# The last unit's softmax sums in four column tiles, with reciprocals spread by transfers

## The chip, the cores and the metric

The kernel runs on one core of one Trainium2 chip. Time is device time in microseconds (us) of one launch; a kernel's time is the median of its runs. Besides, one execution was recorded by the hardware profiler; its rows give start and length of every instruction. The engines are named as the profile names them: PE is TensorE (PEld its weight loads), ACT is ScalarE, DVE is VectorE, POOL is GpSimd, SP is the sequencer that issues most DMAs.

## The reference

Attention with normalised q and k, and behind it a two-layer network with a leaky ReLU. 8 batches, 12 heads, 448 rows, 64 columns; the network takes 3584 tokens of width 768 to 2048 and back.

```python
def _attn_ref(q, k, v, g_q, g_k):
    def rmsnorm(x, g):
        rms = np.sqrt(np.mean(x * x, axis=-1, keepdims=True) + 1e-06)
        return x / rms * g
    q_n, k_n = (rmsnorm(q, g_q), rmsnorm(k, g_k))
    scores = (1.0 / np.sqrt(q.shape[-1])) * np.matmul(q_n, k_n.transpose(0, 1, 3, 2))
    scores = scores - np.max(scores, axis=-1, keepdims=True)
    attn = np.exp(scores)
    attn = attn / (np.sum(attn, axis=-1, keepdims=True) + 1e-09)
    return np.matmul(attn, v)

def _moe_ref(x, w_in, w_out):
    h = x @ w_in
    g = np.maximum(0.01 * h, h)
    return g @ w_out
```

Inputs and outputs are float32; x is the attention's output with the heads of a token side by side.

## The kernel before

The attention is cut into 24 units, each one batch and four of its twelve heads: unit u is group u % 3 of batch u // 3. A unit's scores are computed transposed in seven steps of 64x64 tiles (`qk`, L195), and ScalarE turns each step into exponentials `et` in fp16 (`ex`, L214). Two results are then taken from `et`: the softmax sums and the products with v. Each unit writes its third of `xts[b]`, the network's input x for its batch.

There are two ways to the sums and reciprocals.

- The wide way (units 0 to 3 and the last one, 23): `zsum_slot` (L265) multiplies `et` by ones in 64x64 tiles, 28 matmuls of 448 columns, so that the sums come out already repeated over the 64 rows of each head; `zinv` (L326, L327) takes logarithm and exponential with a minus sign on 128x896; `xmul` (L349) multiplies by the products straight out of PSUM on VectorE, in two halves.
- The narrow way (units 4 to 22): `zcol` (L283) takes 28 matmuls of 224 columns in four column tiles of 32, so that each sum stands in 16 rows only; `zcol_ln` (L300) and `zcol_inv` (L305) work on 128x224; four DMAs on SP (L310) then repeat the reciprocals `zs` over the rows of `rz`; `pv_out` (L295) copies the products from PSUM to `x32`, and `xmul_pool` (L320) multiplies `x32` by `rz` on GpSimd (`xmul_sb` is the same multiply on VectorE).

The network's work stands in `queue`, a list of items (a closure and a cost each). Between the attention's steps `fill` runs items by cost. Each batch adds its items with `push`. After the last unit all that is left is run in order. An item may leave VectorE or ScalarE work for afterwards with `later`; the next item begins with `flush`, which emits it, so such work stands on its engine behind the item's own matmuls.

Around the end the order on PE is this: the first four items i0 to i3 of `seven`, which computes two tiles of batch 6's output by seven products instead of eight (L444, eight matmuls each, most with an add or copy by VectorE or ScalarE behind them), the last unit's sums and products, items i4, i5, i6, and then batch 7 with `late1`, which does the like for the first layer (L564). Its items (n, s), six matmuls each, run in the order of `LATE_ALL`:

```python
    LATE_ALL = ((1, 0), (2, 0), (7, 0), (1, 1), (6, 0), (7, 1), (1, 2), (5, 0), (4, 0), (6, 1), (3, 0), (2, 1), (7, 2), (5, 1),
```

Item n = 1 reads x of the older units only, n = 2 and n = 3 read the last unit's x, n = 4 to 7 read the sums `xs[4]`, `xs[1]`, `xs[2]`, `xs[3]`. VectorE makes those in `x_sum` (L550): 3 and 1 first, then 2 and 4; 2 needs 1, and 4 needs 2. Behind the items VectorE and ScalarE add up the parts (L577, L612, L581) and apply the leaky ReLU (L574). Item (6, 0) accumulates into the PSUM bank of (1, 0), VectorE adds that bank to the one of (7, 0), and (5, 0) accumulates into the same bank again:

```python
            elif n == 6:
                mm(g[1, s], 6, s, xs[2], False)
                later(lambda: vadd(g[7, s][:, 0:S], g[1, s], tmp["v"][:, s % 2]))
            elif n == 5:
                mm(g[1, s], 5, s, xs[1], False)
```

PSUM has four banks for all this (`aux`, handed round in a list while `hold` is on) and two slots of two banks for scores, which `late1` takes over, one bank of each.

Of the kernel before, what the change touches and what calls it, by code (L numbers as in the profile page):

```python
# [18 lines left out]
def kernel(  # L19
# [13 lines left out]
    B, H, S, D = q.shape  # L33
# [4 lines left out]
    NU = B * NQ  # L38
# [18 lines left out]
    def aux(shape, dtype, name):  # L57
        if held:
            return held[0].pop(0)
        return psum.tile(shape, dtype, tag="aux", bufs=4, name=name)  # L60
# [6 lines left out]
    def drop(bank):  # L67
        if held:
            held[0].append(bank)
# [119 lines left out]
    def slot():  # L189
        return psum.tile([P, 2, 512], FP32, tag="sT", bufs=2, name="sT")  # L190
# [69 lines left out]
    def zsum(u, t0=0, t1=NS):  # L260
        s = st[u]
        for t in range(t0, t1):
            for r in range(2):
                for a in range(2):
                    nc.tensor.matmul(s["zt"][r][64 * a:64 * a + 64, 0:S], ones16[64 * r:64 * r + 64],  # L265
                                     s["et"][64 * r:64 * r + 64, t, a], start=(t == 0), stop=(t == NS - 1))

    def zsum_slot(u):
        s = st[u]
        s["zslot"] = slot()  # L270
        s["zt"] = [s["zslot"][:, r] for r in range(2)]
        zsum(u)
# [3 lines left out]
    def zcol(u):  # L276
        s = st[u]
        s["zc"] = aux([P, 512], FP32, "zc")
        for t in range(NS):
            for y in range(2):  # L280
                for a in range(2):
                    c = 32 * (2 * y + a)
                    nc.tensor.matmul(s["zc"][c:c + 32, 0:HS], onesr, s["et"][:, t, a, HS * y:HS * y + HS],  # L283
                                     start=(t == 0), stop=(t == NS - 1))

    def pv_slot(u):
        s = st[u]
        s["pslot"] = slot()
        s["pv"] = [s["pslot"][:, r] for r in range(2)]
        pv(u)  # L290

    def pv_out(u):
        s = st[u]
        s["x32"] = zpool.tile([P, 2, S], FP32, tag="x32", name="x32")
        nc.scalar.copy(s["x32"], s["pslot"][:, :, 0:S])  # L295

    def zcol_ln(u):
        s = st[u]
        s["zs"] = zpool.tile([P, HS], FP32, tag="zs", name="zs")
        nc.scalar.activation(s["zs"], s["zc"][:, 0:HS], AF.Ln)  # L300
        drop(s["zc"])

    def zcol_inv(u):
        s = st[u]
        nc.scalar.activation(s["zs"], s["zs"], AF.Exp, bias=0.0, scale=-1.0)  # L305
        s["rz"] = zpool.tile([P, 2, S], FP32, tag="rz", name="rz")
        for r in range(2):
            for y in range(2):
                src = s["zs"][64 * y + r:64 * y + 64:2, None, :]
                nc.sync.dma_start(s["rz"][:, r, HS * y:HS * y + HS], src.broadcast_to([32, 4, HS]))  # L310

    def xmul_sb(u):
        xmul_pool(u, nc.vector)

    def xmul_pool(u, eng=nc.gpsimd):
        s = st[u]
        b, g = divmod(u, NQ)
        if b not in xts:
            xts[b] = xpool.tile([P, NQ, 2, S], FP16, tag="xt", name="xt")
        eng.tensor_tensor(xts[b][:, g], s["x32"], s["rz"], op=ALU.mult)  # L320

    def zinv(u):
        s = st[u]
        s["rz"] = zpool.tile([P, 2, S], FP32, tag="rz", name="rz")
        if "zslot" in s:
            nc.scalar.activation(s["rz"], s["zslot"][:, :, 0:S], AF.Ln)  # L326
            nc.scalar.activation(s["rz"], s["rz"], AF.Exp, bias=0.0, scale=-1.0)  # L327
        else:
            for r in range(2):
                nc.scalar.activation(s["rz"][:, r], s["zt"][r][:, 0:S], AF.Ln)  # L330
                nc.scalar.activation(s["rz"][:, r], s["rz"][:, r], AF.Exp, bias=0.0, scale=-1.0)

    def pv(u, t0=0, t1=NS):
        s = st[u]
        if t0 == 0 and "pslot" not in s:
            s["pv"] = [aux([P, 512], FP32, "pv") for r in range(2)]
        for t in range(t0, t1):
            for r in range(2):
                for a in range(2):
                    nc.tensor.matmul(s["pv"][r][64 * a:64 * a + 64, 0:S], vts[u % NV][64 * r:64 * r + 64, a, t],  # L340
                                     s["et"][64 * r:64 * r + 64, t, a], start=(t == 0), stop=(t == NS - 1))

    def xmul(u):
        s = st[u]
        b, g = divmod(u, NQ)
        if b not in xts:
            xts[b] = xpool.tile([P, NQ, 2, S], FP16, tag="xt", name="xt")
        for r in range(2):
            nc.vector.tensor_tensor(xts[b][:, g, r], s["pv"][r][:, 0:S], s["rz"][:, r], op=ALU.mult)  # L349
            drop(s["pv"][r])  # L350
# [85 lines left out]
    def later(fn, *args):  # L436
        pend.append(lambda: fn(*args))
# [97 lines left out]
    def x_b(b, i, j):  # L535
        v_ = xts[b].rearrange("p g r (t x) -> p (g r) t x", t=NS)
        return v_[:, HK * i:HK * i + HK, :, 32 * j:32 * j + 32]

    def x_tiles():
        if not xs:  # L540
            two = [prep_p.tile([P, 2, HK, HX], FP16, tag="sq", bufs=3, name="xs") for i in range(2)]
            for n in range(1, 5):
                xs[n] = two[n // 3][:, (n - 1) % 2].rearrange("p k (t x) -> p k t x", t=NS)

    def x_sum(b, n):
        x_tiles()
        t = xs
        a, c = {1: (x_b(b, 0, 1), x_b(b, 0, 0)), 2: (x_b(b, 1, 1), t[1]),
                3: (x_b(b, 1, 1), x_b(b, 0, 1)), 4: (x_b(b, 1, 0), t[2])}[n]
        nc.vector.tensor_tensor(t[n], a, c, op=ALU.subtract)  # L550
# [87 lines left out]
    queue = []  # L638

    def also(fn, *more):  # L640
        def both():
            fn()
            for m in more:
                m()
        return both
# [56 lines left out]
    def fill(u, d, jobs):  # L702
        total = sum(c for c, _ in queue)
        left = WD[d] + 3.0
        uu, dd = u, d
        while True:
            dd += 1
            if dd == 4:
                uu, dd = uu + 1, 0
            if uu == NU or (fed(uu, dd) and (u > 3 or uu > 3)):  # L710
                break
            left += WD[dd]
        debt[0] += total * WD[d] / left
        while queue and debt[0] >= queue[0][0] * 0.5:
            c, fn = queue.pop(0)
            fn()
            debt[0] -= c
            if jobs:
                jobs.pop(0)()
        flush()  # L720
        for job in jobs:
            job()
# [21 lines left out]
    with tc.manual_schedule():  # L744
# [182 lines left out]
        for u in range(3, NU):  # L927
            for d in range(4):
# [75 lines left out]
                    for ti in range(2):  # L1004
                        job(prep_sq, u + 3, ALL, (ti,))
                fill(u, d, jobs)
        zsum_slot(NU - 1)
        pv(NU - 1)
        zinv(NU - 1)
        xmul(NU - 1)  # L1010
        for i, ns in enumerate(((3, 1), (2, 4))):
            c, fn = queue[i]
            queue[i] = (c, also(fn, *[lambda n=n: later(x_sum, B - 1, n) for n in ns]))
        push(B - 1)
        while queue:
            queue.pop(0)[1]()
# [29 lines left out]
```

## Time and profile before

| | us |
|---|---|
| median of 8 runs | 421.68 |
| lowest and highest run | 420.77, 422.46 |
| the profiled execution's own time | 421.3 |
| its span, first to last instruction | 419.5 |
| TensorE busy | 403.2 (96%) |
| ScalarE busy | 303.8 (72%) |
| VectorE busy | 270.2 (64%) |
| granted TensorE clock | 1.0 |

A row of a timeline gives the start from the span's beginning, the length, the engine, the line of the kernel, the operation, what it writes and reads, shapes, and how many instructions are merged in the row. Brackets give idle time of the engine just ahead and what ended it. Rows of TensorE overlap a little, since matmuls are pipelined; the distance from one row's start to the next is what a group costs. "SPq" rows are DMA issues: their length is the sequencer's time, and not the transfer's.

### The profile page before, as it was taken

What the parts mean: (1) busy time and instruction counts of PE and PEld (TensorE: products, weight loads), DVE (VectorE), ACT (ScalarE), POOL (GpSimd) and SP (SyncE); (2) the same over time, 40 slices, a digit from 0 to 9 for tenths busy, and PEclk for the clock granted to TensorE, in tenths of its full rate; (3) what the DMA queues carried; (4) which work ended last, traced back from release to release, by engine and by line L of the source; (5) the groups of instructions that cost most, each with busy time, mean ns of one, the idle gap of its engine ahead of it and who ended that gap; (6) DMA issues with size and microseconds to landing.
All of it is one profiled execution on the core that took longest, in us unless ns stands there. A gap on an engine that the chain in (4) does not pass through costs nothing.

```text
span 419.5 us, 9568 instructions
## 1 busy us (share of the span) xinstructions
PE 403.2 (96%) x3959; PEld 222.9 (53%) x3959; DVE 270.2 (64%) x440; ACT 303.8 (72%) x474; POOL 83.1 (20%) x75
## 2 busy tenths in 40 slices
PE   8787999999999999999999999999999999999995
PEld 7454444545445544555455544455445557558863
DVE  5888675887568837566448735467338787527762
ACT  5999877768887689767986779967986657653600
POOL 1968422200020112210121120120101101010000
PEclk9999999999999999999999999999999999999999
DMA  7999997889664795677664796578552460032023
GB/s 262 226 251 256 238 251 115 208 151 211 157 155 74 215 236 104 162 182 166 154 140 91 204 202 143 157 147 179 163 108 44 121 157 8 8 76 75 2 53 99
DMA packets 71951, 62.42 MB, mean 149 GB/s; under 512 B 36324, under 2 KB 67044, under 8 KB 71908
## 3 DMA queue, kind: packets, MB, share of 16 engines
q1 hardware_dynamic: 61312, 49.62, 46.2%
q0 software_dynamic: 10272, 11.80, 17.7%
q8 instruction: 31, 0.51, 0.5%
q10 hardware_dynamic: 324, 0.39, 0.3%
q14 instruction: 12, 0.10, 0.1%
HBM read 45.61 MB, written 11.01 MB: 135 GB/s over the span
## 4 chain that ended last, share of the span: by engine, by line
PE 83%; ACT 9%; DVE 6%; issue 1%; DVEq 0%; ACTq 0%
PE hps L362 27%; PE sT L195 8%; PE sT L340 6%; ACT et L214 6%; PE ma L444 5%; PE md L444 5%; PE mc L444 5%; PE bank L444 5%; PE bank L564 4%; PE op L403 3%; PE zc L283 3%; PE mb L444 3%; PE warm L742 2%; PE sT L444 2%; DVE n L167 1%
## 5 line engine op out<-in xcount | busy, mean ns | idle before, releaser
L214 ACT ACTIVATE et<-sT,eb 128x896 f16<-128x896 f32 x166 | 159.6, 1011 | 18.6 <-PE sT L195 16.8
L362 PE MATMUL hps<-xt,win 128*128 128x448 f16 x600 | 120.8, 353 | 0.2 <-DVE xt L349 0.2
L362 PEld LDWEIGHTS <-win 128*128 128x128 f16 x612 | 56.8, 98 | 58.2 <-issue 9.6
L320 POOL TENSOR_TENSOR xt<-x,rz 128x896 f16<-128x896 f32 x16 | 33.4, 2085 | 148.7 <-DMA rz<-zs 131.5
L167 DVE TENSOR_TENSOR n<-rq,rinv 128x896 f16<-128x896 f32 (+2 forms) x25 | 28.1, 1127 | 49.7 <-ACT rinv L161 47.0
L356 ACT ACTIVATE gt<-hps 128x448 f16<-128x448 f32 x100 | 54.1, 557 | 6.0 <-PE hps L362 5.4
L195 PE MATMUL sT<-qkT 64*64 64x448 f16 x664 | 52.4, 363 | 4.6 <-ACT et L214 3.6
L155 DVE TENSOR_REDUCE ssq<-sq 128x14 f32<-128x896 f32 (+2 forms) x49 | 50.4, 1058 | 1.1 <-ACT sq L144 1.1
L444 PEld LDWEIGHTS <-sa 128*128 128x128 f16 x352 | 32.8, 98 | 26.3 <-issue 6.1
L295 ACT COPY x<-sT 128x896 f32<-128x896 f32 x19 | 17.2, 906 | 36.4 <-DVE sT L245 36.4
L124 POOL DMA_DIRECT2D vt<-in_v_dram x24 | 18.2, 759 | 114.2 <-PE sT L340 106.7
L195 PEld LDWEIGHTS <-qkT 64*64 64x64 f16 x672 | 15.5, 104 | 37.8 <-issue 34.2
L444 PEld LDWEIGHTS <-gt 128*128 128x128 f16 x264 | 25.2, 98 | 18.8 <-issue 2.4
L340 PE MATMUL sT<-et,vt 64*64 64x448 f16 x532 | 28.5, 349 | 0.3
L403 PE MATMUL op<-wout,gt 128*128 128x384 f16 x160 | 28.4, 327 | 0.0
L340 PEld LDWEIGHTS <-vt 64*64 64x64 f16 x672 | 20.7, 107 | 11.3 <-issue 1.7
L232 DVE TENSOR_REDUCE sT<-sT 128x1 f32<-128x896 f32 x22 | 24.0, 1093 | 4.0 <-PE sT L195 4.0
L167 DVE TENSOR_TENSOR n<-rk,rinv 128x896 f16<-128x896 f32 (+2 forms) x26 | 26.1, 1011 | 0.0
L403 PEld LDWEIGHTS <-gt 128*128 128x128 f16 x192 | 17.6, 98 | 14.3 <-issue 3.0
L444 PE MATMUL ma<-wout,gt 128*128 128x384 f16 x128 | 23.5, 326 | 0.0
L425 DVE TENSOR_TENSOR sa<-gt 128x512 f16<-128x512 f16 (+1 forms) x15 | 8.2, 544 | 18.6 <-ACT gt L356 14.0
L144 ACT ACTIVATE sq<-rq 128x896 f32<-128x896 f32 (+2 forms) x18 | 16.3, 913 | 1.0 <-DMA rq<-in_q_dram 1.0
(135 smaller groups left out, 515.9 us busy)
## 6 DMA issues: line engine op xcount, KB each, us to landing
rq<-in_q_dram SPq DMA_DIRECT2D x24, 448.0 KB, 3.8
rk<-in_k_dram SPq DMA_DIRECT2D x24, 448.0 KB, 5.1
out_dram<-ost SPq DMA_DIRECT2D x52, 192.0 KB, 3.3
rz<-zs SPq DMA_DIRECT2D x76, 112.0 KB, 2.3
vt<-in_v_dram POOLq DMA_DIRECT2D x24, 224.0 KB, 5.3
win<-in_moe_w_in_dram POOLq DMA_DIRECT2D x8, 384.0 KB, 14.9
wout<-in_moe_w_out_dram POOLq DMA_DIRECT2D x2, 1536.0 KB, 27.6
out_dram<-ost SPq DMA_DIRECT2D x4, 96.0 KB, 2.1
```

Source lines behind the costliest of these rows:

```text
L124: nc.gpsimd.dma_start(vts[u % NV].rearrange("p a t d -> p a (t d)"), rows(v, u))
L155: nc.vector.tensor_reduce(buf(u, "ssq")[:, ti, :, c[0]:c[1]], buf(u, f"sq{ti}")[:, :, c[0]:c[1]], axis=AXL.X, op=ALU.add)
L167: nc.vector.tensor_tensor(buf(u, "n16")[:, ti, c[0]:c[1]].rearrange("p s a d -> p a s d"), src[:, :, c[0]:c[1]], buf(u, "rinv")[:, ti, :, ...
L195: nc.tensor.matmul(banks[a][64 * r:64 * r + 64, 0:S].rearrange("p (t x) -> p t x", t=NS), kT(u, r, a, t), qT(u, r, a), start=True, stop=True)
L214: nc.scalar.activation(s["et"][:, t], sT[:, :, 0:S], AF.Exp, bias=s["eb"], scale=1.0)
L232: nc.vector.tensor_reduce(s["spare"][:, 511:512], sT[:, :, 0:S], axis=AXL.XY, op=ALU.max)
L320: eng.tensor_tensor(xts[b][:, g], s["x32"], s["rz"], op=ALU.mult)
L340: nc.tensor.matmul(s["pv"][r][64 * a:64 * a + 64, 0:S], vts[u % NV][64 * r:64 * r + 64, a, t], s["et"][64 * r:64 * r + 64, t, a], start=(t ...
L356: nc.scalar.activation(dst, src, AF.Prelu, bias=0.0, scale=1.0, alpha=0.01)
L362: nc.tensor.matmul(hps[:, 0:S], win16[:, kt // 2, kt % 2, ts(ft, P)], xt[:, kt // 2, kt % 2], start=(kt == 0), stop=(kt == KT - 1))
L403: nc.tensor.matmul(op2[:, 0:HC], gt[:, ft, ds(col(t), P)], wout16[:, ft, ds(HC * half, HC)], start=(ft == 0), stop=(ft == FT - 1))
L444: nc.tensor.matmul(bank[:, 0:HC], a[:, f], b[:, f], start=(first and f == 0), stop=(f == HF - 1), skip_group_check=not first)
```

## The change

The last unit's sums take the narrow way: `zcol`, `zcol_ln`, `zcol_inv` with its four DMAs, the products into a PSUM slot and by `pv_out` into SBUF. The multiply `xmul_sb` runs on VectorE, and is emitted behind the first of the items that follow; the sums `x_sum` move one item back each.

```diff
-        zsum_slot(NU - 1)
-        pv(NU - 1)
-        zinv(NU - 1)
-        xmul(NU - 1)
-        for i, ns in enumerate(((3, 1), (2, 4))):
+        zcol(NU - 1)
+        zcol_ln(NU - 1)
+        zcol_inv(NU - 1)
+        pv_slot(NU - 1)
+        pv_out(NU - 1)
+        for i, fns in enumerate(([lambda: xmul_sb(NU - 1)], [lambda n=n: x_sum(B - 1, n) for n in (3, 1)], [lambda n=n: x_sum(B - 1, n) for n in (2, 4)])):
             c, fn = queue[i]
-            queue[i] = (c, also(fn, *[lambda n=n: later(x_sum, B - 1, n) for n in ns]))
+            queue[i] = (c, also(fn, *[lambda f=f: later(f) for f in fns]))
         push(B - 1)
         while queue:
             queue.pop(0)[1]()
```

## The prediction

> **What bounds the kernel now.** I read the busy shares first, then the chain that ended last, then the timeline of the tail, engine by engine.
>
> ```profile
> PE 403.2 (96%) x3959; PEld 222.9 (53%) x3959; DVE 270.2 (64%) x440; ACT 303.8 (72%) x474; POOL 83.1 (20%) x75
> PE 83%; ACT 9%; DVE 6%; issue 1%; DVEq 0%; ACTq 0%
> ```
>
> TensorE is busy 96% of the span and carries 83% of the chain, so a microsecond on its path counts in full. The changed place is near 374 us. TensorE's timeline there (start, length, line, count):
>
> ```profile
> 373.78 1.52 PE L265 MATMUL sT<-et,ones 64*64 64x448 f16 x28
> 375.13 1.49 PE L340 MATMUL bank<-et,vt 64*64 64x448 f16 x28
> 376.55 1.47 PE L444 MATMUL bank<-tw,sa 128*128 128x384 f16 x8
> ...
> 380.46 1.31 PE L564 MATMUL bank<-xt,win 128*128 128x224 f16 x12
> 381.61 0.74 PE L564 MATMUL bank<-xs,win 128*128 128x224 f16 x6
> 382.19 0.74 PE L564 MATMUL bank<-xt,win 128*128 128x224 f16 x6
> 382.76 0.74 PE L564 MATMUL bank<-xs,ws 128*128 128x224 f16 x6
> ...
> 384.49 0.74 PE L564 MATMUL bank<-xs,ws 128*128 128x224 f16 x6
> ```
>
> From 373.78 on nothing stands idle: sums (L265), products with v (L340), three items of the second product (L444 at 376.55, 377.86, 379.16), then late1's items of six matmuls every 0.575 us. (1,0) starts at 380.46 and needs only older units; (2,0) at 381.04 reads the last unit's x; (7,0) at 381.61 reads xs 3, (6,0) at 382.76 reads xs 2, (5,0) at 384.49 reads xs 1. From there to the last matmul the only gap is 0.21 us (at 397.9), so delay here is not won back. What feeds the items now:
>
> ```profile
> 376.35 0.95 ACT L327 ACTIVATE rz<-rz 128x896 f32<-128x896 f32 x1
> 377.33 1.16 DVE L349 TENSOR_TENSOR xt<-bank,rz 128x448 f16<-128x448 f32 x2 [2.88 <-ACT rz L327]
> 378.87 0.92 DVE L550 TENSOR_TENSOR xs<-xt 128x672 f16<-128x672 f16 x2
> 380.17 1.04 DVE L550 TENSOR_TENSOR xs<-xt,xs 128x672 f16<-128x672 f16 x2
> 383.54 0.63 DVE L577 TENSOR_TENSOR bank<-bank,v 128x448 f32<-128x448 f32 x1 [0.50 <-PE bank L564]
> ```
>
> x is there at 378.49, 2.5 us before (2,0) wants it. The tightest place is the last row: the VectorE add of (6,0)'s bank ends at 384.17, and (5,0), which accumulates into that same bank, starts at 384.49. Slack there is 0.32 us. Last, how the units ahead do it (unit 22):
>
> ```profile
> 357.09 0.85 PE L283 MATMUL bank<-et,onesr 128*32 128x224 f16 x28
> 357.88 0.23 PE L244 MATMUL sT<-dg,onesp 128*128 128x64 f16 x2
> 365.08 0.39 ACT L305 ACTIVATE zs<-zs 128x224 f32<-128x224 f32 x1
> 365.53 2.46 SPq L310 DMA_DIRECT2D rz<-zs  x4
> 369.91 2.08 POOL L320 TENSOR_TENSOR xt<-x,rz 128x896 f16<-128x896 f32 x1 [20.77 <-DMA rz<-zs]
> ```
>
> The narrow sums take 0.79 us to the next group's start; but between the end of the reciprocals (365.47) and the multiply (369.91) lie 4.44 us of transfers. POOL was waiting for nothing else.
>
> **TensorE.** 28 matmuls with a step of 375.13 - 373.78 = 1.35 us give way to 28 with a step of 0.79: 0.56 us saved. The order is otherwise unchanged; the 28 products write a PSUM slot instead of two aux banks, and keep 376.55 - 375.13 = 1.42. The rows hold no change from 128*128 or 128*32 tiles straight to 64*64 in this order; by the neighbouring gaps (0.18 to 0.36 us, already inside these steps) it is worth between -0.15 and +0.15; I take 0. So, undisturbed: products 374.57, the three items 375.99, 377.29, 378.60, (1,0) 379.90, (2,0) 380.47, (7,0) 381.05, (6,0) 382.20, (5,0) 383.93. [...]
>
> **ScalarE.** Out go L326 and L327 on 128x896 (0.92 and 0.95), in come the logarithm (0.36), the reciprocal (0.39 to 0.41) and a copy of the products (0.91). Idle before (2.1 us) and after (3.9 us) covers that. Sums end at 373.78 + 0.85 = 374.63; ScalarE starts 0.10 later (as 375.30 to 375.40 now); a dependent step adds 0.03: reciprocals done at 374.73 + 0.36 + 0.03 + 0.41 = 375.53. The copy waits for the products and is done near 377.0, under the transfers.
>
> **Transfers.** Four more issues on SP. They stand behind two output stores that leave at 368.7, so nothing holds them; the later stores queue behind them with microseconds to spare and are worth 0. From reciprocals to multiply, the units where POOL was waiting show 4.43, 4.48, 4.40, 4.43, 4.42, 4.48, 4.43, 4.44 us, whether the DMA engines were quiet or not: four issues in 2.5 us, and 2.2 to 2.3 from the last issue to its landing. So the multiply starts at S = 375.53 + 4.44 = 379.97. [...]
>
> **VectorE, where it is paid.** Its order becomes: add of the first item, multiply (L320), add of the second item, xs 3 and xs 1, add of the third, xs 2 and xs 4, then late1's adds. The multiply waits for the transfers, and all that follows is queued behind it, with VectorE idle before. Steps from S, each the distance to the next start in the rows of now: multiply 1.00 (the VectorE form of L320, 1.08 long, frees the engine after 1.00 at 84.96); add 0.47 (378.40 to 378.87); two sums 0.83; add 0.47; two sums 0.96 (380.17 to 381.13); add for (2,0) 0.55; copy for (7,0) with its dependent follower 0.61 + 0.04; add of (6,0)'s bank 0.63. Sum 5.56, and 0.06 until TensorE moves (43.67 to 43.73 for another wait of that kind). (5,0) can start at 379.97 + 5.62 = 385.59.
>
> On the way (2,0) stalls to S + 1.14 = 381.11 at its second matmul, (7,0) to 381.96 (xs 3), (1,1) to 382.88, because its bank is freed only by the third item's add, (6,0) follows at 383.46, (7,1) and (1,2) run on, and (5,0) would come at 385.18 but waits until 385.59. Before it started at 384.49: 1.10 us later. TensorE's stalls are 385.59 - 383.93 = 1.66, less the 0.56 saved. After (5,0) VectorE's next add needs (5,0) itself, so both are back in the old rhythm and the shift stays 1.10 to the end; ScalarE's copies for (1,1) and (1,2), queued behind the add for (2,0), are done by 385.9, ahead of the items that need them.
>
> **Sum.** The profiled execution took 421.3 (span 419.5, 1.8 around it). 421.3 + 1.10 = 422.4. The median of the runs is 421.68, 0.38 above that execution, so I expect a median of 422.8. About 0.2%, 0.84 us, is what a measurement here can tell from no change.
>
> **Rivals.** (a) The transfers land as one, not as four in a row: then S = 375.53 + 0.06 + 2.3 = 377.9, (5,0) is ready at 383.5, before 383.93, no item waits, and 0.56 is kept: 420.7, a median of 421.1. It decides from S at or below 378.3, that is 2.8 us after the reciprocals. For it speaks that a single landing is 2.3; against it, eight units between 4.40 and 4.48. Chance 0.08. (b) Half of the delay: the tail moves little data, VectorE may be released sooner than POOL was, and each tenth at S is a tenth of the time. With S 0.3 to 0.9 earlier the change costs 0.2 to 0.8: a median of 421.9 to 422.5. Against it: unit 22's 4.44 fell in a stretch as quiet. Chance 0.18. (c) A slow landing: L310's landings show min 2.2, median 2.3, max 4.3; with 4.3, S and the end are 2.0 later: 424.4, median 424.8. Against it: 4.3 fell near 150 us, amid loads, and late in the tail little is moved (the page's GB/s row shows 2 in one slice). Chance 0.09. The forecast has 0.65.
>
> **How the numbers follow.** The forecast's own spread is 0.2 for S, 0.15 for the mode changes and VectorE's steps, and 0.3 for the runs: 422.3 to 423.3. To hold 8 in 10 the range takes in (b) and the near ends of the others: 421.4 to 423.9, leaving out (a) and most of (c). Faster by over 0.84 us is more than the 0.56 that can be saved at all: 0.03 for what I do not see. Within: (a), most of (b) and a sixth of the forecast, 0.29. Slower 0.68.
>
> **What would show it.** In the changed profile: sums of 0.8 us at 373.8; reciprocals done near 375.5; a VectorE L320 near 380.0 that names the transfer as releaser after about 2 us idle; idle of some 0.4 us each ahead of TensorE's items between 380.5 and 385.6; the first item that reads xs 1 near 385.6; from there every row 1.1 later than now. I am wrong if L320 starts before 378.5, if TensorE runs through without waiting, or if the shift after 386 is not the one at (5,0).

## The result, and the profile after

The changed kernel takes 423.62 us in the median of 12 runs (422.93 to 425.68), against 421.71 us for the kernel before in runs beside it (33 runs). The ratio is 1.0049, with a 95% interval of 1.0038 to 1.0061: 2.1 us slower, between 1.6 and 2.6. Forecast was 422.8 us, 1.1 slower.

The profiled execution took 425.68 us, the longest of the 12, with a span of 423.9. A part of that excess is not the change's: the sums, ahead of which the two kernels have the same code, begin at 374.91 instead of 373.78. The difference arises in the first 12 us: at 9.44 TensorE has waited 1.24 us for VectorE (L167), a wait that the profile of before does not have. The granted clock over the first 20 us, 0.91 here and 1.00 there, is not the cause, since it falls only behind that wait, at 13.06, and the lag hardly grows from there. In the profiles of all kernels below, the sums begin anywhere between 373.7 and 377.0. So I compare traces by one distance that does not contain the start: from the first matmul of the sums to the first matmul of item (5,0), the first that reads `xs[1]`. In the kernel before it is 384.49 - 373.78 = 10.71 us. After it is 389.11 - 374.91 = 14.20, which is 3.49 more; the forecast had 1.10 more.

First the page of the changed kernel, its line of busy times and its chain by engine:

```profile
PE 405.8 (96%) x3959; PEld 223.8 (53%) x3959; DVE 270.0 (64%) x439; ACT 303.6 (72%) x475; POOL 83.0 (20%) x75
PE 79%; ACT 9%; DVE 7%; issue 2%; DMA 2%; SPq 1%; DVEq 0%; ACTq 0%
```

The same number of matmuls keep TensorE busy 2.6 us longer, although the sums became cheaper: this profile has two stretches of 3.41 us at half the clock (0.50), from 13.06 and, as will be seen, from 385.12 in the tail. The chain now has DMA and SP's queue in it, which it did not have before. Next the timeline of the tail (start, length, engine, line, count, and in brackets the idle time ahead with what ended it):

```profile
374.91 0.85 PE L283 MATMUL bank<-et,onesr 128*32 128x224 f16 x28
375.69 1.52 PE L340 MATMUL sT<-et,vt 64*64 64x448 f16 x28
376.25 0.39 ACT L305 ACTIVATE zs<-zs 128x224 f32<-128x224 f32 x1
376.70 3.77 SPq L310 DMA_DIRECT2D rz<-zs  x4
377.14 1.47 PE L444 MATMUL bank<-tw,sa 128*128 128x384 f16 x8
377.31 0.91 ACT L295 COPY x<-sT 128x896 f32<-128x896 f32 x1 [0.67 <-PE sT L340]
381.05 0.83 PE L564 MATMUL bank<-xt,win 128*128 128x224 f16 x7
382.31 1.09 DVE L320 TENSOR_TENSOR xt<-x,rz 128x896 f16<-128x896 f32 x1 [3.10 <-DMA rz<-zs]
383.45 0.64 PE L564 MATMUL bank<-xt,win 128*128 128x224 f16 x5 [1.56 <-DVE xt L320]
384.34 0.73 PE L564 MATMUL bank<-xs,win 128*128 128x224 f16 x6 [0.25 <-DVE xs L550]
385.22 1.28 PE L564 MATMUL bank<-xt,win 128*128 128x224 f16 x6
386.29 1.32 PE L564 MATMUL bank<-xs,ws 128*128 128x224 f16 x6
389.11 0.74 PE L564 MATMUL bank<-xs,ws 128*128 128x224 f16 x6
```

Down to the copy (L295) this is the forecast: sums in 0.78, products in 1.45, reciprocals done 1.73 us after the sums began. Then three things are to be seen. The row of the four transfers is 3.77 us long, where unit 22's in the kernel before was 2.46. The multiply (L320) so starts 5.67 us after the end of the reciprocals, at 376.64, and not 4.44. And from 385.22 an item of six matmuls takes 1.1 us to the next one's start, and not 0.575. The chain that ended last, in order of time, names the first of these:

```profile
377.32 1.87 SPq L310
379.87 2.31 DMA rz<-zs
382.31 1.09 DVE xt L320
```

One issue took 1.87 us; the landing of the last transfer, 2.31, is what was forecast. The slow items are the clock. Windows of 1 us (stretch, length, busy time and count of PE, PEld, DVE, ACT and POOL; then the granted clock, the DMA share and GB/s):

```profile
385.00:386.00 1.00, 0.85 (x6) 0.62 (x5) 0.97 (x3) 0.00 (x0) 0.00 (x0) 0.56 0.94 197
386.00:387.00 1.00, 1.00 (x7) 0.80 (x6) 1.00 (x3) 0.30 (x1) 0.00 (x0) 0.50 1.02 301
387.00:388.00 1.00, 1.00 (x8) 0.76 (x7) 0.54 (x2) 0.69 (x2) 0.00 (x0) 0.50 0.83 240
388.00:389.00 1.00, 1.00 (x9) 0.88 (x8) 0.55 (x2) 0.00 (x0) 0.00 (x0) 0.73 0.14 49
```

After its wait of 1.56 us and the short ones behind it TensorE ran at half its clock for about 3.4 us (385.1 to 388.5).

### The profile page after: what moved, and what is told of

Its sections match the earlier page's. It is cut to its first block, busy times and chain, and to the rows that moved or that the text cites. A ratio compares the mean times of both kernels' runs of the same rounds, so it can differ in the third digit from the quotient of the medians.

```text
span 423.9 us, 9575 instructions
## 1 busy us (share of the span) xinstructions
PE 405.8 (96%) x3959; PEld 223.8 (53%) x3959; DVE 270.0 (64%) x439; ACT 303.6 (72%) x475; POOL 83.0 (20%) x75
## 4 chain that ended last, share of the span: by engine, by line
PE 79%; ACT 9%; DVE 7%; issue 2%; DMA 2%; SPq 1%; DVEq 0%; ACTq 0%
PE hps L362 27%; PE sT L195 8%; PE sT L340 6%; ACT et L214 5%; PE ma L444 5%; PE md L444 5%; PE mc L444 5%; PE bank L564 4%; PE bank L444 4%; PE op L403 3%; PE zc L283 3%; PE mb L444 3%; DVE n L167 2%; PE sT L444 2%; DMA rk<-in_k_dram 1%
## 5 line engine op out<-in xcount | busy, mean ns | idle before, releaser
L320 POOL TENSOR_TENSOR xt<-x,rz 128x896 f16<-128x896 f32 x16 | 33.3, 2081 | 148.8 <-DMA rz<-zs 140.3
L167 DVE TENSOR_TENSOR n<-rq,rinv 128x896 f16<-128x896 f32 (+2 forms) x25 | 27.8, 1116 | 49.7 <-ACT rinv L161 47.0
L295 ACT COPY x<-sT 128x896 f32<-128x896 f32 x20 | 18.1, 906 | 37.1 <-DVE sT L245 36.5
L340 PE MATMUL sT<-et,vt 64*64 64x448 f16 x560 | 30.0, 350 | 0.3
L167 DVE TENSOR_TENSOR n<-rk,rinv 128x896 f16<-128x896 f32 (+2 forms) x26 | 26.1, 1011 | 0.0
L144 ACT ACTIVATE sq<-rk 128x896 f32<-128x896 f32 x17 | 16.3, 958 | 1.7 <-DMA rk<-in_k_dram 1.7
```

The source lines that it names most:

```text
L167: nc.vector.tensor_tensor(buf(u, "n16")[:, ti, c[0]:c[1]].rearrange("p s a d -> p a s d"), src[:, :, c[0]:c[1]], buf(u, "rinv")[:, ti, :, ...
```

## The experiments

The theories at the start: the forecast's own (four issues in a row, then VectorE's chain up to (5,0)), with the additions that SP's issue was held up by a fetch of TensorE's instructions, and that the clock's fall belongs to the cost; against it, that the narrow sums or the later place of the multiply cost something by themselves, or that the transfers are late for another reason. The table puts all profiles side by side: "wait" is from the end of the reciprocals to the start of the multiply, "stretch" is from the first matmul of the sums to that of (5,0), with its difference from 10.71. Ratios stand with their 95% intervals.

| kernel | wait | stretch | ratio to the kernel before | median |
|---|---|---|---|---|
| after | 5.67 | 14.20 (+3.49) | 1.0049 [1.0038, 1.0061] | 423.62 |
| e1_again | 5.31 | 12.72 (+2.01) | 1.0048 [1.0028, 1.0068] | 424.10 |
| e2_no_transfer | - | 10.18 (-0.53) | 0.9973 [0.9961, 0.9984] | 421.16 |
| e7_wide_moved | - | 10.71 (0) | 0.9998 [0.9982, 1.0014] | 422.13 |
| e3_fetch | 4.41 | 11.82 (+1.11) | 1.0033 [1.0019, 1.0048] | 423.57 |
| e3b_fetch_before | - | 10.71 (0) | 1.0010 [0.9995, 1.0024] | 422.29 |
| e9_fetch_before | - | 10.71 (0) | 1.0001 [0.9989, 1.0012] | 421.58 |
| e10_fetch_after | 4.39 | 11.81 (+1.10) | 1.0023 [1.0011, 1.0035] | 422.60 |
| e4_two_queues | 4.68 | 12.09 (+1.38) | 1.0026 [1.0008, 1.0044] | 423.12 |
| e5_chain | 5.31 | 11.98 (+1.27) | 1.0027 [1.0014, 1.0041] | 422.81 |
| e8_combined | 3.84 | 10.51 (-0.20) | 1.0007 [0.9994, 1.0020] | 422.14 |
| e11_best | 3.81 | 10.27 (-0.44) | 0.9986 [0.9975, 0.9997] | 420.85 |
| e12_double | 7.75 | 16.31 (+5.60) | 1.0124 [1.0110, 1.0139] | 426.86 |

### The changed kernel again

e1_again is the changed kernel without an edit.

> The changed kernel once more, with its clock. Theory A (what the first profile shows is the rule): of the four reciprocal transfers one issue on SP is again about 1.2 us too long, because TensorE's instructions are being fetched at that moment; the multiply starts 5.7 us after the reciprocals and not 4.44, and TensorE's clock falls to half for 3.4 us after its waits. Then the time is 1.0045 of before. Theory B (the first profile was an odd execution): 4.44 us, no fall of the clock, and 1.0026 of before, 1.1 us more.

The stretch is 2.01 longer than before, and 1.48 shorter than in the first profile: this time the clock did not fall. The wait is 5.31, and again the second of the four issues is long. The rows of the four issues (shortest, median and longest in ns, and the first and last start):

```profile
L310 SPq DMA_DIRECT2D rz<-zs x4: 565/600/1519, 375.7 to 378.5; - x4
```

The DMA view of the same stretch lists one packet on a queue that has nothing to do with the kernel's data:

```profile
q8 instruction: 1, 0.02, 1.7%
```

It begins at 376.48, and the long issue at 376.31. In the first profile the two are at 377.41 and 377.32. The queue's share of the 16 engines gives the packet's length: 0.96 us here, and 1.38 us in the first profile, where the DMA view of the four issues (4.0 us) has

```profile
q8 instruction: 1, 0.02, 2.2%
```

So the longer fetch has the longer issue, 1.87 us against 1.52, and that is, to 0.01, the difference between the two waits, 5.67 and 5.31. Over the whole execution this queue has 31 packets of 16 KB, and TensorE has 7918 matmuls and weight loads, so I take a packet for a fetch of TensorE's instructions, on average one to 255 of them; the rows do not name the engine that a packet serves. It comes near the same place of the program each time: 2.4 to 2.6 us after the start of the sums in the profiles of after, e1_again, e5_chain and e12_double, and 3.1 in that of e4_two_queues.

The kernel before has such a meeting too, with a fetch from 230.94 and an issue of 1256 ns, in a unit where GpSimd does wait for the transfers:

```profile
229.95 0.39 ACT L305 ACTIVATE zs<-zs 128x224 f32<-128x224 f32 x1
230.40 3.14 SPq L310 DMA_DIRECT2D rz<-zs  x4
235.54 2.07 POOL L320 TENSOR_TENSOR xt<-x,rz 128x896 f16<-128x896 f32 x1 [7.99 <-DMA rz<-zs]
```

From the end of the reciprocals (230.34) to the multiply (235.54) are 5.20 us. The forecast's list of waits does not have this one.

### Without the transfers

e2_no_transfer takes the four transfers away.

```diff
         s["rz"] = zpool.tile([P, 2, S], FP32, tag="rz", name="rz")
+        if u == NU - 1:
+            s["rz"] = s["x32"] = zpool.tile([P, 2, S], FP32, tag="x32", name="x32")
+            return
         for r in range(2):
```

> The four transfers of the last unit are left out, and its multiply takes the copied products twice instead of products and reciprocals. Theory A (the loss is all in the wait for the transfers, and what the narrow sums save is real): the multiply starts at about 377.1 on before's time scale, no item of late1 waits, the clock stays at 1, and the kernel is 0.56 us faster than before, ratio 0.9987. Rival (the narrow sums in front of 64x64 products cost a mode change, or the two more tiles on PSUM slots cost a wait): 1.000 or above.

TensorE's timeline of e2_no_transfer, from the sums to the first reader of x and to (5,0):

```profile
374.15 0.85 PE L283 MATMUL bank<-et,onesr 128*32 128x224 f16 x28
380.30 1.31 PE L568 MATMUL bank<-xt,win 128*128 128x224 f16 x12
384.33 0.74 PE L568 MATMUL bank<-xs,ws 128*128 128x224 f16 x6
```

Twelve matmuls in one row at 380.30: (2,0) follows (1,0) without a wait. The stretch is 10.18, 0.53 shorter than before, against 0.56 in the forecast's term for TensorE. All else that the changed kernel loses comes through the transfers. The ratio says 1.1 us faster, 0.7 to 1.6, which is more than the trace's 0.53 even at its near end. I have no row that explains the rest; the kernel before had a median of 422.24 in the runs beside this one, higher than beside any other.

### The wide sums at the new place

e7_wide_moved keeps the new order on VectorE, the PSUM slot and the copy, and takes the wide sums and reciprocals.

```diff
-        zcol(NU - 1)
-        zcol_ln(NU - 1)
-        zcol_inv(NU - 1)
+        zsum_slot(NU - 1)
+        zinv(NU - 1)
         pv_slot(NU - 1)
```

> One part alone: sums and reciprocals stay wide and on ScalarE as before, but the products go to SBUF, and the multiply on VectorE and the sums of x stand where the changed kernel has them. Theory A (the late order by itself is harmless, the wait for the transfers is the loss): ScalarE is done with reciprocals and copy at about 378.2, the multiply starts there, 378.25 + 5.62 = 383.9 is before the 384.49 at which (5,0) stands anyway, and the ratio is 1.000. Rival (the additions queued behind a later multiply are a loss by themselves): (5,0) waits, 1.001 to 1.002.

The multiply starts at 378.80 and the stretch is 10.71, to the hundredth that of before. So moving the multiply and the sums `x_sum` one item back, and the copy by ScalarE, cost nothing while x is there in time. With e2_no_transfer this leaves the transfers as the only cause.

### The fetch moved away

e3_fetch puts 56 tiny matmuls (112 instructions of TensorE) near the start of the kernel, so that the fetches come at other places; e3b_fetch_before does the same to the kernel before, to price the edit.

```diff
+    def tiny(n, bank):
+        for x in range(n):
+            nc.tensor.matmul(bank[:, P:P + 16], onesp, onesp[:, 0:16], start=True, stop=True)
...
         warm(12, wb)
+        tiny(14, wb)
...
```

> The changed kernel with 56 matmuls of 16 columns more, in the first 20 us, where TensorE waits anyway: they move every later fetch of TensorE's instructions 112 instructions earlier in the program. Theory A (the fetch that falls on the transfers' issues lengthens one): the fetch is over before the first issue, all four issues take 0.52 to 0.61 us, the multiply starts 4.44 us after the reciprocals, and the time is about 1.2 us or less below the changed kernel's, ratio to before 1.0020 to 1.0030. Rival (the long issue is due to SP's long idle time or to the transfers themselves): an issue is as long as in the changed kernel, and the ratio stays at 1.0045.

> The kernel before with the same 56 small matmuls in the first 20 us: the control for the run with the moved fetch. Theory A (they lie in TensorE's waits and cost nothing; before, nothing waits for a transfer in the tail): 1.000 of before, within 0.001. Rival (they lengthen the start or move some other fetch onto a needed transfer): above 1.001, and the gain in the run with the moved fetch was larger than its ratio says.

The wait is 4.41 and the stretch +1.11. But the ratio of e3b_fetch_before, 1.0010 [0.9995, 1.0024], leaves open whether the tiny matmuls cost 0.4 us at the start or nothing, so the ratio of e3_fetch decides little. I therefore moved the fetch in a way that adds nothing: the warm-up matmuls near the start become half as many and twice as wide, which takes out 130 instructions.

```diff
     def warm(n, bank):
-        for x in range(n):
-            nc.tensor.matmul(bank[:, P:2 * P], onesp, onesp, start=True, stop=True)
+        for x in range(n // 2):
+            nc.tensor.matmul(bank[:, P:3 * P], onesp, onesw, start=True, stop=True)
```

`onesw` is a tile of ones twice as wide as `onesp`. e9_fetch_before has this edit on the kernel before, e10_fetch_after on the changed one.

> The kernel before, with the warm-up matmuls of the start half as many and twice as wide (256 columns, the same TensorE time): 130 instructions fewer ahead of the tail, so that every later fetch falls at another place, and no work added. Control for the next two runs. Theory A: 1.000 of before, within 0.001, since nothing in before's tail waits for a transfer. Rival (the start or a fetch elsewhere matters): off by more.

> The changed kernel with the same wider warm-ups, nothing else. Theory A (what the prediction missed is the fetch among the four issues, and only that): no issue above 0.65 us, the multiply 4.4 us after the reciprocals, (5,0) 1.1 us later against the start of the sums than before, ratio 1.0026. Rival (the rest of the loss is TensorE's clock or the start): the ratio stays at 1.0045 to 1.005.

On the kernel before the edit is worth nothing: 1.0001 [0.9989, 1.0012], and the same stretch. On the changed kernel the longest of the four issues is 603 ns, and the DMA view of this stretch shows no packet of q8:

```profile
L311 SPq DMA_DIRECT2D rz<-zs x4: 564/598/603, 376.1 to 378.0; - x4
```

The timeline of e10_fetch_after:

```profile
374.32 0.85 PE L284 MATMUL bank<-et,onesr 128*32 128x224 f16 x28
380.45 1.09 DVE L321 TENSOR_TENSOR xt<-x,rz 128x896 f16<-128x896 f32 x1 [1.82 <-DMA rz<-zs]
380.47 0.83 PE L565 MATMUL bank<-xt,win 128*128 128x224 f16 x7
381.60 0.64 PE L565 MATMUL bank<-xt,win 128*128 128x224 f16 x5 [0.29 <-DVE xt L321]
382.48 0.73 PE L565 MATMUL bank<-xs,win 128*128 128x224 f16 x6 [0.25 <-DVE xs L551]
386.13 0.74 PE L565 MATMUL bank<-xs,ws 128*128 128x224 f16 x6 [0.30 <-DVE bank L578]
```

The multiply comes 4.39 us after the reciprocals, (2,0) stops for 0.29 after its first matmul, and (5,0) waits 0.30 for VectorE's add: the picture of the forecast. Its stretch is 1.10 longer than before, the forecast's own number, and the ratio gives 1.0 us (0.5 to 1.5). The fetch is worth 2.01 - 1.10 = 0.91 in the traces.

### Two queues

e4_two_queues issues two of the four transfers on ScalarE's queue.

```diff
-                nc.sync.dma_start(s["rz"][:, r, HS * y:HS * y + HS], src.broadcast_to([32, 4, HS]))
+                eng = nc.scalar if u == NU - 1 and y else nc.sync
+                eng.dma_start(s["rz"][:, r, HS * y:HS * y + HS], src.broadcast_to([32, 4, HS]))
```

> Of the last unit's four transfers two go through ScalarE's queue, two through SP's. Theory A (every tenth by which the transfers land earlier is a tenth of the time, until VectorE's chain is no longer late): two issues in a row instead of four, the multiply about 3.2 us after the reciprocals, at 378.7 on before's scale; the add of (6,0)'s bank then holds (5,0) up to 384.3 at most, against 384.49 before: ratio 0.9995 to 1.001. Rival (the issue is bound by something that both queues share, or the loss lies elsewhere in the tail): the multiply still 4.4 us or more after the reciprocals, ratio 1.0025 or above.

The wait is 4.68, not 3.3. In the DMA view of that stretch the fetch is there again, this time (379.73 to 380.7) while the data move, and the transfers of both queues take 3.6 and 3.9 us from issue to landing, where e11_best, without a fetch, has 2.4 and 2.8:

```profile
q8 instruction: 1, 0.02, 1.4%
rz<-zs SPq DMA_DIRECT2D x2, 112.0 KB, 3.6
rz<-zs ACTq DMA_DIRECT2D x2, 112.0 KB, 3.9
```

Without the fetch, in e8_combined and e11_best below, two queues have 3.84 and 3.81. So the fetch costs 0.85 here too, and two queues in place of one save 4.39 - 3.81 = 0.58, less than I thought. By its numbers e4_two_queues came out on the rival's side (4.4 us or more, 1.0025 or above), and the fetch explains that only in part. ScalarE's two issues take 1.47 us in a row where SP's two take 1.21 (1.48 and 1.21 in e11_best). That the fetch is what lengthens the landings fits its time and the difference; no run moved it to other places within the transfers.

### A shorter chain on VectorE

e5_chain emits the multiply behind the second item, so that the add of the second item goes ahead of it into VectorE's idle time, gives the copy for (7,0) to ScalarE, and moves (2,0)'s ScalarE work (`out_`) behind that copy.

```diff
-        for i, fns in enumerate(([lambda: xmul_sb(NU - 1)], [lambda n=n: x_sum(B - 1, n) for n in (3, 1)], ...
+        for i, fns in enumerate(([], [lambda: xmul_sb(NU - 1)] + [lambda n=n: x_sum(B - 1, n) for n in (3, 1)], ...
...
-                later(lambda: nc.vector.tensor_copy(tmp["v"][:, s % 2], g[7, s][:, 0:S]))
+                if tail and s == 0:
+                    later(lambda: nc.scalar.copy(tmp["v"][:, 0], g[7, s][:, 0:S]))
```

> The changed kernel with VectorE's chain shortened: the add of the second item stands ahead of the multiply instead of behind it (0.47 less behind the wait), and the first copy for (7,0) goes to ScalarE, ahead of its leaky ReLU of (2,0) (0.55 to 0.65 less). The transfers stay as late as they are, 5.3 us with the lengthened issue. Theory A (TensorE waits for that chain at (5,0), step for step): (5,0) at S + 4.6 instead of S + 5.62, the time 1.0 us below the changed kernel's, ratio to before 1.0024. Rival (TensorE is held by the landing alone, at (2,0) and (7,0), and the rest runs on behind it): 0.3 us or less, ratio 1.004 or more.

With the same wait as e1_again, 5.31, the stretch is 0.74 shorter, where I expected 1.0. TensorE's timeline of e5_chain shows what came next:

```profile
382.13 0.64 PE L564 MATMUL bank<-xt,win 128*128 128x224 f16 x5 [1.20 <-DVE xt L320]
383.63 0.73 PE L564 MATMUL bank<-xt,win 128*128 128x224 f16 x6 [0.15 <-DVE ost L451]
385.93 0.74 PE L564 MATMUL bank<-xs,ws 128*128 128x224 f16 x6
```

Nothing waits for VectorE ahead of (5,0) any more. What is left is (1,1), which waits for the third item's add (L451) to free its PSUM bank, an add that still stands behind the multiply; from there on TensorE runs without a wait.

### All three, and a version that beats both

e8_combined joins e3_fetch, e4_two_queues and e5_chain.

> All three at once: the fetch moved by 56 small matmuls at the start, two of four transfers on ScalarE's queue, the shortened chain. Theory A: without a fetch among the transfers the two queues land them about 3.3 us after the reciprocals, the multiply starts at 378.8 on before's scale, (5,0) could start at 383.4 and stands at 383.9, so nothing waits, the 0.56 us of the narrow sums is kept: ratio 0.9987, faster than both. Rival (two queues do not shorten the landing even without the fetch): the multiply 4.4 us or more after the reciprocals, (5,0) at 384.5, ratio 1.000.

The multiply comes 3.84 us after the reciprocals, not 3.3. The stretch is 0.20 shorter than before, and the time is that of before, 1.0007 [0.9994, 1.0020], with the tiny matmuls in it. (1,1) still waits 0.15 for its bank. e11_best takes the wide warm-ups in place of the tiny matmuls, puts (1,1) ahead of (2,0), since it reads older units only, and puts all the sums `x_sum` behind the third item, so that its add comes ahead of them.

```diff
-    LATE_ALL = ((1, 0), (2, 0), (7, 0), (1, 1), (6, 0),
+    LATE_ALL = ((1, 0), (1, 1), (2, 0), (7, 0), (6, 0),
...
+        for i, fns in enumerate(([], [lambda: xmul_sb(NU - 1)], [lambda n=n: x_sum(B - 1, n) for n in (3, 1, 2, 4)])):
```

> The narrow sums kept, and their wait covered: wider warm-ups (the fetch is out of the way), two of four transfers on ScalarE's queue, the add of the second item ahead of the multiply and that of the third right behind it, the first copy for (7,0) on ScalarE, and item (1,1), which needs only the older units, ahead of (2,0). Theory A: the multiply at 3.8 us after the reciprocals, at 379.4 on before's scale; (2,0) has 0.575 us more in front of it, (7,0) has xs 3 at 381.4 and stands at 381.6, (5,0) could start at 383.9; nothing waits, 0.56 us less than before, ratio 0.9987. Rival (a wait takes the place of the one removed: ScalarE's two issues hold its copy of the products, or the moved item its bank): 1.000 or more.

The timeline of e11_best:

```profile
374.38 0.85 PE L284 MATMUL bank<-et,onesr 128*32 128x224 f16 x28
376.17 1.21 SPq L312 DMA_DIRECT2D rz<-zs  x2
376.19 1.48 ACTq L312 DMA_DIRECT2D rz<-zs  x2
379.92 1.09 DVE L322 TENSOR_TENSOR xt<-x,rz 128x896 f16<-128x896 f32 x1
380.52 1.89 PE L566 MATMUL bank<-xt,win 128*128 128x224 f16 x18
382.25 0.74 PE L566 MATMUL bank<-xs,win 128*128 128x224 f16 x6
384.65 0.74 PE L566 MATMUL bank<-xs,ws 128*128 128x224 f16 x6
```

The two queues issue side by side, and 18 matmuls stand in one row at 380.52: (1,1) fills the time until x is there. The stretch is 0.44 shorter than before, of 0.53 that can be had, and the time is 0.9986 [0.9975, 0.9997], 0.6 us faster (0.1 to 1.1). It beats the kernel before by a little and the changed one by 2.7 us, the difference of the two ratios (0.0063 of 422), each taken against the kernel before and not side by side.

### Four transfers more

e12_double puts four more transfers of the same kind, into a tile that nobody reads, ahead of the four on SP.

```diff
+        if u == NU - 1:
+            other = epool.tile([P, 2, S], FP32, tag="et", name="other")
+            for r in range(2):
+                for y in range(2):
+                    src = s["zs"][64 * y + r:64 * y + 64:2, None, :]
+                    nc.sync.dma_start(other[:, r, HS * y:HS * y + HS], src.broadcast_to([32, 4, HS]))
```

> The changed kernel with the suspected cost doubled: ahead of the four transfers four more of the same kind to a tile that nobody reads. Theory A: the multiply 2.5 us later than in the changed kernel, about 7.8 us after the reciprocals; TensorE waits 4 us in one piece, (5,0) comes 2.5 us later still, 4.5 us later than before against the start of the sums, and after so long a wait TensorE's clock is at half for a few us in every execution, 1.2 us more: ratio 1.011 to 1.014. Rival (the landing is not what TensorE waits for): 1.005. Rival on the clock (the fall in the first profile has nothing to do with the wait): clock 1 in the tail, 1.011.

The wait grows from 5.31 to 7.75, by 2.44 for four more issues, or 0.61 each; in both a fetch lengthens one issue (here to 1.39 us, among the four added ones). The time grows by more: the stretch is 3.59 longer than that of e1_again. The timeline of e12_double:

```profile
383.14 1.09 DVE L326 TENSOR_TENSOR xt<-x,rz 128x896 f16<-128x896 f32 x1 [5.18 <-DMA rz<-zs]
384.29 0.64 PE L570 MATMUL bank<-xt,win 128*128 128x224 f16 x5 [3.65 <-DVE xt L326]
389.96 0.74 PE L570 MATMUL bank<-xs,ws 128*128 128x224 f16 x6
```

(5,0) comes 6.82 us after the multiply, and in e1_again 5.68. The difference, 1.14, is the clock. Windows of e12_double, the granted clock third from the right:

```profile
386.00:387.00 1.00, 0.94 (x6) 0.75 (x6) 0.96 (x4) 0.00 (x0) 0.00 (x0) 0.50 0.93 215
387.00:388.00 1.00, 1.00 (x7) 0.80 (x6) 1.00 (x2) 0.47 (x1) 0.00 (x0) 0.50 1.08 289
388.00:389.00 1.00, 1.00 (x8) 0.76 (x7) 0.54 (x2) 0.53 (x2) 0.00 (x0) 0.50 0.77 249
```

It is the same picture as in the first profile of the changed kernel, where (5,0) came 6.80 after the multiply, 1.12 more than in e1_again.

## Why the prediction was right, and where it was off

**Right in the mechanism and in the range, short in size.** TensorE waits at the places that were named, and 423.62 lies in the stated range of 421.4 to 423.9. It lies above the spread that the forecast gave itself, 422.3 to 423.3: the range held because it had been widened for the rivals, and what used that room, a late issue, was none of them. That is luck.

**The sum holds.** With the forecast's 1.10 for a wait of 4.44, each trace that has the changed order of work gives 1.10, plus its wait less 4.44, plus the clock's fall where there is one. In the first four rows this tests that VectorE's chain from the multiply to (5,0) is the same whatever the wait. The clock's terms, 1.12 and 1.14, are what that chain takes more than in e1_again, so the last two rows fit by construction:

| kernel | 1.10 + (wait - 4.44) + clock | measured |
|---|---|---|
| e10_fetch_after | 1.10 - 0.05 = 1.05 | 1.10 |
| e3_fetch | 1.10 - 0.03 = 1.07 | 1.11 |
| e4_two_queues | 1.10 + 0.24 = 1.34 | 1.38 |
| e1_again | 1.10 + 0.87 = 1.97 | 2.01 |
| after | 1.10 + 1.23 + 1.12 = 3.45 | 3.49 |
| e12_double | 1.10 + 3.31 + 1.14 = 5.55 | 5.60 |

**TensorE's 0.56** is 0.53 (e2_no_transfer). The steps are 0.78 for the sums and 1.45 for the products, where the forecast had 0.79 and 1.42: the change from 128*32 straight to 64*64 costs 0.03 that was put at 0, inside the 0.15 either way that was allowed for it.

**ScalarE and the later order** cost nothing, as said: reciprocals were done 1.73 to 1.74 us after the start of the sums in all traces with narrow sums (forecast 1.75), the copy ran under the transfers, and e7_wide_moved has exactly the stretch of before.

**The term that was mis-sized is S**, the reciprocals plus 4.44. It was plus 5.31 and 5.67 in the two profiles of the changed kernel. The step took 4.44 from eight units whose waits agreed to 0.08, and took that as the price wherever it is paid. But the eight were not all: in the profile of before there are 14 units in which POOL stood idle until the transfers landed. Thirteen of these waits are 4.35 to 4.52, and the fourteenth is the 5.20 shown above, the one whose issues a fetch met. With 5.20 the same sum would have given 1.86, against 2.01 in e1_again. At the last unit the fetch meets the issues in both profiles of the changed kernel. Rival (c), a slow landing, was too large (2.0 more) and wrong in place: the last landing took 2.31, and the issue was late. Rivals (a) and (b) fall with e10_fetch_after, whose wait is 4.39: the four issues do follow one another, and VectorE is released no sooner than POOL was. A landing of 2.31 is what the rows of before had, 2.2 to 2.3, and as those rows had said, the issues come on top.

**VectorE's chain**, S + 5.62, is 5.68 in e1_again and in e10_fetch_after. On the way, e1_again has (2,0)'s second matmul at S + 1.15 (forecast 1.14), (7,0) at S + 2.03 (1.99) and (1,1) at S + 2.92 (2.91).

**The clock** was not in the sum. Where it fell in the tail, that cost 1.1 us more. In e1_again, e3_fetch, e4_two_queues, e5_chain and e10_fetch_after it did not fall there; the longest wait there was 1.21 us, in e1_again. The mechanism (1.10) and the fetch (0.91) make 2.0, and the ratio of the changed kernel says 2.1 (1.6 to 2.6); so there the fall can come in about half of the executions at most, and how often it does stays open. For e12_double the ratio says 5.2 (4.6 to 5.9), where the sum is 5.6 with a fall and 4.5 without: there the fall seems to be the rule. No run filled the wait with matmuls that do nothing, so whether the fall then stays away is not shown.

## What to carry to other kernels

A transfer through SBUF that replaced a wider computation cost its chain here (four issues in a row and one landing, 4.4 us), and the 0.5 us saved on the busiest engine is only kept if so much other work, on every engine that the chain holds up, lies between it and its first reader. Before a price is taken from places that agree, list every place of the kind: here thirteen agreed, and the fourteenth, 0.8 us dearer, showed what the changed place would pay. Ask what met the dearest one, since it may come back: the fetch here began 2.4 to 3.1 us after the start of the sums in all five profiles listed above. Before giving up a change of this sort, look for work that depends on nothing new and put it under the wait; here, with the fetch out of the way, one item moved forward, a second queue and a shorter VectorE chain turned 1.0 us lost into 0.6 gained.

## What the runs showed of the hardware that was not expected

**A fetch of instructions held up a DMA issue.** In the places shown here SP's issue of a transfer took 1.26 (before), 1.39 (e12_double), 1.50 (e5_chain), 1.52 (e1_again) and 1.87 us (after) where a 16 KB packet of q8, taken above for a fetch for TensorE, 0.93 to 0.96 long and in the last case 1.38, began near it. With the fetch moved (e3_fetch, e10_fetch_after) it was 0.56 to 0.62 for all four. The rest of the record agrees: the 14 profiles have 1098 such issues on SP, 35 of them are longer than 0.66 us, up to 2.05, and every one of the 35 overlaps a fetch. The reverse does not hold: 28 others overlap one and stay short. Where the fetch came during the landing (e4_two_queues), the wait was longer by 0.85.

**TensorE's clock fell to half after waits, though not after all of them.** It did so for about 3.4 us after a wait of 3.65 us (e12_double) and, in one profile of the changed kernel, after 1.56 us with short waits behind it. In the clock record of that profile the falls at 13.06 and at 385.12 last 3.413 us each, and from the end of the first to the second are 368.64 us, 108 times that length. In the 3.41 us ahead of the fall in the tail TensorE was busy for 1.55 us in that profile and for 1.37 in e12_double. In e1_again stretches of 3.413 us, laid on from the first entry of its clock record (6.39), cut the tail's waits in two, with 2.43 and 2.79 us busy, and the clock stayed. A guess from these few numbers is that the fall depends on how the waits lie to such stretches, which differs between executions. No run shows that, and one stretch speaks against its being all: e12_double has 3.41 us with 1.47 us busy, just ahead of those with 1.37, that no fall follows.
